# Local attention in pairs of 58-query blocks on half the partitions, in natural row order

## The chip, the cores and the metric

The kernel runs on one core of one Trainium2 chip. The metric is the time of one execution on the device in microseconds (us). The clock that the chip grants to TensorE varies from run to run (1.00 is the full clock). An execution that is more than 1.5% above the fastest of its kernel is called slow. The engines are PE (TensorE), DVE (VectorE), ACT (ScalarE), POOL (GpSimd) and SP, which here only issues transfers.

## The reference

```python
# q, k, v: 8 batches x 8 heads x 576 rows x 64, float32
q_d, k_d, v_d = means of q, k, v over groups of 4 rows          # 144 coarse rows
out_up    = repeat(softmax(q_d k_d^T / 8) v_d, 4)               # coarse attention
mask      = abs(i - j) < 4
out_local = softmax(where(mask, q k^T / 8, -1e9)) v             # local attention
x         = (out_up + out_local) as 8 x 576 x 512
wq, wk    = x @ w_q, x @ w_k                                    # 512 -> 64
mixed     = (wq wk^T / 8) x
out       = relu(mixed) @ w_out                                 # 8 x 576 x 512
```

## The kernel before

Eight batches go through four software stages: *cast* (to fp16, on POOL), *a* (transposes, coarse sums, local scores), *b* (probabilities times v, coarse attention, adding the two), *c* (the mixer, done as (x wq)(wk^T x), and the output product). Stages c, b and a of three successive batches, and the cast of the next, are interleaved in one program, and a scheduler orders each engine's instructions.

The queries are split into blocks of 120 rows, each with the 128 keys that it needs. The block's rows lie in *phase order*: all rows 0 mod 4 first, then 1 mod 4, and so on, so that one coarse row serves four stretches of the block.

```python
TQ = [30, 30, 30, 30, 24]; QN = [4 * t for t in TQ]; KS = [0, 116, 236, 356, 448]
# setup: masks, pooling matrices and selectors, with affine selects on GpSimd
for n in (0, 1, 4):                                  # one mask serves blocks 1, 2, 3
    asel(m3, [[-1, 4], [-4, TQ[n]]], ALU.is_ge, 0.0, OFF[n] + 3, 1)
    asel(m3, [[1, 4], [4, TQ[n]]], ALU.is_ge, 0.0, 3 - OFF[n], -1)
for n in (0, 1, 4): ...                              # P likewise: two selects each
for n in range(NW): asel(sel[n] ..., ALU.not_equal, 1.0, ...)    # one select each
[...]
def evac():                                          # q's transposed copy: DVE
    nc.vector.tensor_copy(qT[:, :, :, 0:128], pq16 ...)          # 4 phases x 144
def evack():                                         # k's: ACT, natural order
    nc.scalar.copy(kT[:, :, 0:512] ..., pk16 ...)
[...]
def sums():                                          # GpSimd
    nc.gpsimd.tensor_tensor(tq, qT[:, :, 0:2, :], qT[:, :, 2:4, :], op=ALU.add)
    nc.gpsimd.tensor_tensor(qd, tq[:, :, 0, :], tq[:, :, 1, :], op=ALU.add)
    nc.gpsimd.tensor_tensor(tk, k4[:, :, :, 0:2], k4[:, :, :, 2:4], op=ALU.add)
    ...                                              # kd from tk: five small adds
def score(n):                                        # five blocks
    for hl in range(NP):
        for p in range(2):                           # 64x128 weights, 120 columns
            nc.tensor.matmul(p_[:, p, hl * W:(hl + 1) * W],
                             kT[64 * p:64 * p + 64, hl, KS[n]:KS[n] + 128],
                             qT[64 * p:64 * p + 64, hl, :, 30 * n:30 * n + TQ[n]], ...)
    nc.scalar.activation(e_, p_[:, :, 0:4 * W], ACTF.Exp, scale=s_local)
    nc.vector.tensor_tensor(e8, e8, mask_n broadcast over 8 heads, op=ALU.mult)
[...]
def og(i):                                           # output, two of these a batch
    c = 120 * (2 * i + ff)
    nc.tensor.matmul(p_[0:120, ff, :], rmx[:, r, c:c + 120], wo16[:, r, :], ...)
    [...]                                            # copy, then DMA of 4-row groups
```

The *mask product* is `E = E * mask` on DVE, two operands in SBUF, 960 columns (768 in the last block), five times a batch.

The softmax here doesn't subtract the row's maximum and nothing guards it: scores larger than these inputs give would overflow.

Of the kernel before, what the change touches and what calls it, by code (L numbers as in the profile page):

```python
# [19 lines left out]
def kernel(  # L20
# [20 lines left out]

    NW = 5
    TQ = [30, 30, 30, 30, 24]
    QN = [4 * t for t in TQ]
    KS = [0, 116, 236, 356, 448]
    OFF = [KS[n] - 120 * n for n in range(NW)]

# [18 lines left out]
    def load(b):  # L66
# [10 lines left out]
        for n in range(NW):  # L77
            nc.sync.dma_start(v32[:, n], _ap(vb, KS[n] * D, [[D, 128], [S * D, H], [1, D]]))
# [16 lines left out]
    for n in (0, 1, 4):  # L95
        t_ = cst.tile([128, QN[n]], FP16, name=f"mask{n}")
        nc.vector.memset(t_, 1.0)
        m3 = t_.rearrange("p (f t) -> p f t", f=4)
        asel(m3, [[-1, 4], [-4, TQ[n]]], ALU.is_ge, 0.0, OFF[n] + 3, 1)
        asel(m3, [[1, 4], [4, TQ[n]]], ALU.is_ge, 0.0, 3 - OFF[n], -1)  # L100
        masks[n] = t_
# [3 lines left out]
    P = {}  # L105
    for n in (0, 1, 4):
        t_ = cst.tile([128, 32], FP16, name=f"P{n}")
        nc.vector.memset(t_, 0.0)
        u_ = t_[:, 0:TQ[n]]
        nc.vector.memset(u_, 0.25)  # L110
        asel(u_, [[-4, TQ[n]]], ALU.is_ge, 0.0, OFF[n], 1)
        asel(u_, [[4, TQ[n]]], ALU.is_ge, 0.0, 3 - OFF[n], -1)
        P[n] = t_
    P[2] = P[3] = P[1]
# [7 lines left out]

    sel = []
    for n in range(NW):
        t_ = cst.tile([128, 128], FP16, name=f"sel{n}")
        nc.vector.memset(t_, 0.0)
        asel(t_[:, 0:QN[n]].rearrange("p (f t) -> p f t", f=4), [[0, 4], [-1, TQ[n]]],
             ALU.not_equal, 1.0, 0 if n == 4 else -30 * n, 1)
        sel.append(t_)
# [3 lines left out]
    for i in range(2):  # L133
# [3 lines left out]
        es = []  # L137
        for n in range(NW):
            t_ = cst.tile([128, H * QN[n] + 32], FP16, name=f"E{n}_{i}")
            nc.vector.memset(t_[:, H * QN[n]:], 0.0)  # L140
            es.append(t_)
# [3 lines left out]
        for n in range(4):  # L145
            asel(t_[32 * n:32 * n + 32, :, 64], [[0, H]], ALU.is_ge, 0.0, 29, -1)
# [6 lines left out]
        asel(o_, [[0, 2], [32, 4]], ALU.is_ge, 0.0, 23, -1)  # L153
# [32 lines left out]
    def stage_a(b):  # L186
# [13 lines left out]
        def evac():  # L200
            qT = g["qT"] = big.tile([128, NP, 4, T], FP16, name="qT", tag="qT")
            nc.vector.tensor_copy(qT[:, :, :, 0:128],
                                  g["pq16"].rearrange("p a (j f t) -> p (a j) f t", j=2, f=4))

        def evack():
            kT = g["kT"] = big.tile([128, NP, S], FP16, name="kT", tag="kT")
            nc.scalar.copy(kT[:, :, 0:512].rearrange("p j (t f) -> p j t f", f=4),  # L207
                           g["pk16"].rearrange("p a (j f t) -> p (a j) t f", j=2, f=4))

        def rem():  # L210
            qT, kT = g["qT"], g["kT"]
            pr = ps(FP16, "pr")
            for j in range(NP):
                nc.tensor.transpose(pr[:, 0, 128 * j:128 * j + 128],
                                    g["r16"][:, 2 * j:2 * j + 2, :], id16)
            nc.vector.tensor_copy(qT[:, :, :, 128:T],
                                  _ap(pr, 0, [[row(pr), 128], [128, NP], [1, 4], [4, 16]]))
            nc.scalar.copy(kT[:, :, 512:S], _ap(pr, 64, [[row(pr), 128], [128, NP], [1, 64]]))

        def sums():  # L220
            qT, kT = g["qT"], g["kT"]
            tq = big.tile([128, NP, 2, T], FP32, name="tq", tag="tq", bufs=1)
            qd = g["qd"] = big.tile([128, NP, T], FP16, name="qd", tag="qd")
            nc.gpsimd.tensor_tensor(tq, qT[:, :, 0:2, :], qT[:, :, 2:4, :], op=ALU.add)  # L224
            nc.gpsimd.tensor_tensor(qd, tq[:, :, 0, :], tq[:, :, 1, :], op=ALU.add)  # L225
            tk = big.tile([128, NP, T, 2], FP32, name="tk", tag="tq", bufs=1)
            k4 = kT.rearrange("p j (t f) -> p j t f", f=4)
            kd = kdS[b % 2]
            nc.gpsimd.tensor_tensor(tk, k4[:, :, :, 0:2], k4[:, :, :, 2:4], op=ALU.add)  # L229
            for j in range(NP):  # L230
                nc.gpsimd.tensor_tensor(  # L231
                    kd[:, j, 0:128].rearrange("p (n t) -> p n t", n=4)[:, :, 0:30],
                    tk[:, j, 0:120, 0].rearrange("p (n t) -> p n t", n=4),
                    tk[:, j, 0:120, 1].rearrange("p (n t) -> p n t", n=4), op=ALU.add)
            nc.gpsimd.tensor_tensor(kd[:, :, 128:152], tk[:, :, 120:T, 0], tk[:, :, 120:T, 1],
                                    op=ALU.add)


        def score(n):
            def f_():  # L240
                qT, kT = g["qT"], g["kT"]
                W = QN[n]
                p_ = ps(name="psc")
                for hl in range(NP):
                    for p in range(2):
                        nc.tensor.matmul(p_[:, p, hl * W:(hl + 1) * W],  # L246
                                         kT[64 * p:64 * p + 64, hl, KS[n]:KS[n] + 128],
                                         qT[64 * p:64 * p + 64, hl, :, 30 * n:30 * n + TQ[n]],
                                         start=True, stop=True)
                E = E_S[b % 2][n]  # L250
                e_ = E[:, 0:H * W].rearrange("p (a c) -> p a c", a=2)
                nc.scalar.activation(e_, p_[:, :, 0:4 * W], ACTF.Exp, scale=s_local)  # L252
                e8 = E[:, 0:H * W].rearrange("p (h c) -> p h c", h=H)
                nc.vector.tensor_tensor(  # L254
                    e8, e8, _ap(masks[n], 0, [[row(masks[n]), 128], [0, H], [1, W]]), op=ALU.mult)
            return f_

        def vd():
# [8 lines left out]
            for p in range(2):  # L267
# [4 lines left out]

        return [(.9, tr("q16")), (0, evac), (.9, tr("k16")), (0, evack), (.25, rem), (0, sums),
                (.3, score(0)), (.3, score(1)), (.3, score(2)), (.3, score(3)), (.3, score(4)),
                (.5, vd)]

    def stage_b(b):
# [33 lines left out]
        def ca(i):  # L311
            def f_():
# [5 lines left out]
                lo, hi = ((0, 128), (120, T))[i]  # L318
# [18 lines left out]
        def av(n):  # L337
            def f_():
                if n == 0:
                    g["rz"] = big.tile([128, NW, 2, 4], FP32, name="rz", tag="rz")  # L340
                rz, W, E, v16 = g["rz"], QN[n], E_S[b % 2][n], g["v16"]
                p_ = ps(name="pav")
                for h in range(H):
                    c = ((h % 2) * 4 + h // 2) * W
                    nc.tensor.matmul(p_[:, h // 4, 65 * (h % 4):65 * (h % 4) + 65],  # L345
                                     E[:, c:c + 128], v16[:, n, h, :], start=True, stop=True)
                nc.vector.reciprocal(rz[0:W, n], _ap(p_, 64, [[row(p_), W], [512, 2], [65, 4]]))  # L347
                x_ = g["x"][n] = big.tile([128, DM], FP16, name=f"x{n}", tag=f"x{n}")
                nc.vector.tensor_tensor(
                    _ap(x_, 0, [[row(x_), W], [256, 2], [64, 4], [1, 64]]),  # L350
                    _ap(p_, 0, [[row(p_), W], [512, 2], [65, 4], [1, 64]]),
                    _ap(rz, 8 * n, [[row(rz), W], [4, 2], [1, 4], [0, 64]]), op=ALU.mult)
            return f_

        def up(n):
            def f_():
                W, x_ = QN[n], g["x"][n]
# [3 lines left out]
                nc.vector.tensor_tensor(x_[0:W], x_[0:W], pu[0:W, 0, :], op=ALU.add)  # L361
# [164 lines left out]
```

## Time and profile before

| | before |
|---|---|
| median of 3 runs | 253.94 us (253.6 to 254.33) |
| profiled run | 255.02 us, span 253.3 us, granted clock 0.869 |
| distance between M2 products (one a batch), full batches | 25.7, 25.8, 27.1, 29.0, 25.2 us |
| 40 mask products | 53.3 us |
| first cast of q begins | 7.72 us |

"M2 product" is the first `pm` matmul of a batch on PE. It closes each batch's chain, so the distance from one to the next is the batch's period. The first lies at 57.78 us (the head), the last at 234.67, 18.6 us from the end (the tail).

One batch of before, from its timeline (columns: start us, duration us, engine, line, operation, out<-in, count, and in brackets the idle time before it with what ended it):

```profile
91.42 1.40 POOL L225 TENSOR_TENSOR qd<-tq 128x576 f16<-128x576 f32 x1
91.88 1.45 DVE L254 TENSOR_TENSOR E_1_176<-E_1_176,mask_91 128x960 f16<-128x960 f16 x1 [0.21 <-ACT E_1_176 L252]
...
92.90 2.40 POOL L229 TENSOR_TENSOR tk<-kT 128x1152 f32<-128x1152 f16 x1
...
93.97 1.84 DVE L254 TENSOR_TENSOR E_1_178<-E_1_178,mask_95 128x960 f16<-128x960 f16 x1
...
97.34 2.83 POOL L174 CAST q_1129<-q_1028 128x2048 f16<-128x2048 f32 x1
97.77 0.65 DVE L254 TENSOR_TENSOR E_1_180<-E_1_180,mask_95 128x960 f16<-128x960 f16 x1
...
98.93 1.75 DVE L254 TENSOR_TENSOR E_1_182<-E_1_182,mask_95 128x960 f16<-128x960 f16 x1
...
102.33 0.54 DVE L254 TENSOR_TENSOR E_1_184<-E_1_184,mask_99 128x768 f16<-128x768 f16 x1
...
107.10 0.64 ACT L396 CAST wT<-pw 128x576 f16<-128x576 f32 x1 [0.57 <-PE pw L393]
107.84 1.22 DVE L202 COPY qT<-pq_1454 128x2048 f16<-128x2048 f16 x1 [1.85 <-PE pq_1454 L196]
108.46 0.42 ACT L405 COPY wk<-pwk 96x320 f16<-96x320 f16 x1 [0.72 <-PE pwk L403]
```

The same 960-column product takes 0.65 us or 1.45 to 1.84 us.

### The profile page before, as it was taken

The numbers are of one execution on the slowest core, as the hardware profiler recorded it, in microseconds if no ns is written. First come the engines' busy times: TensorE is split into PE (matmuls) and PEld (weight loads), VectorE is DVE, ScalarE is ACT, GpSimd is POOL, SyncE is SP. The second block draws the span as 40 slices with busy tenths as digits, with TensorE's granted clock in tenths as the row PEclk, the third lists the DMA queues.
The fourth block names the chain that finished last, engine by engine and source line by source line (L and its number), as shares of the span: only waits on it lengthen the run. The fifth ranks groups of instructions, "written<-read, shape, count | busy, mean of one in ns | idle before, by whom it ended". The sixth has DMA issues, their size and how long they took to land.

```text
span 253.3 us, 4685 instructions
## 1 busy us (share of the span) xinstructions
PE 182.3 (72%) x1856; PEld 115.2 (45%) x1856; DVE 177.4 (70%) x320; ACT 110.9 (44%) x153; POOL 137.3 (54%) x140
## 2 busy tenths in 40 slices
PE   0430786498988885888769866887788977996890
PEld 0330563266546643565337533554455544553340
DVE  7148499337895889578995899579977995754210
ACT  2081345035455554556343741556355546212310
POOL 8979939920999099708960599009960920000000
PEclk9995586559589999999799987899999799979568
DMA  6999999999227992699349961797330033024015
GB/s 209 254 241 363 219 241 265 213 306 183 44 78 195 304 194 80 176 310 196 91 111 318 182 160 32 232 263 163 89 100 4 1 97 93 0 44 145 0 25 161
DMA packets 71366, 40.41 MB, mean 160 GB/s; under 512 B 51760, under 2 KB 68144, under 8 KB 71344
## 3 DMA queue, kind: packets, MB, share of 16 engines
q1 hardware_dynamic: 71344, 40.11, 65.8%
q8 instruction: 14, 0.23, 0.4%
q14 instruction: 8, 0.07, 0.1%
HBM read 30.67 MB, written 9.44 MB: 158 GB/s over the span
## 4 chain that ended last, share of the span: by engine, by line
PE 41%; DVE 26%; ACT 13%; POOL 13%; issue 4%; ACTq 0%; POOLq 0%
PE po L448 6%; ACT kT L207 4%; PE pw L393 4%; DVE os L453 3%; PE pol L463 3%; ACT rmx L435 3%; PE px L374 3%; PE pmx L426 2%; DVE E_1_178 L254 2%; POOL tk L229 2%; POOL tq L224 2%; DVE E_1_176 L254 2%; PE pav L345 2%; ACT Ec L295 2%; DVE E_1_182 L254 2%
## 5 line engine op out<-in xcount | busy, mean ns | idle before, releaser
L224 POOL TENSOR_TENSOR tq<-qT 128x1152 f32<-128x1152 f16 x8 | 18.9, 2363 | 64.4 <-DVE rz L347 58.6
L448 PE MATMUL po<-wo_90,rmx 128*120 128x512 f16 x128 | 39.0, 461 | 0.6 <-ACT os L451 0.4
L448 PEld LDWEIGHTS <-rmx 128*120 128x120 f16 x128 | 20.1, 162 | 15.1 <-issue 8.6
L246 PE MATMUL psc<-qT,kT 64*128 64x120 f16 (+1 forms) x320 | 16.2, 228 | 7.3 <-ACT rmx L435 2.5
L229 POOL TENSOR_TENSOR tk<-kT 128x1152 f32<-128x1152 f16 x8 | 19.2, 2400 | 0.6
L246 PEld LDWEIGHTS <-kT 64*128 64x128 f16 x320 | 10.8, 100 | 18.2 <-issue 15.0
L437 DVE TENSOR_SCALAR rmx<-pmx 128x576 f16<-128x576 f32 x16 | 12.0, 748 | 8.4 <-PE pmx L431 8.2
L463 PE MATMUL pol<-wo_90,rmx 128*96 128x512 f16 x32 | 10.1, 408 | 7.7 <-DVE os L453 7.7
L451 ACT COPY os<-po 120x1024 f32<-120x1024 f32 x8 | 8.1, 1012 | 16.3 <-PE po L448 16.3
L393 PE MATMUL pw<-xT,wqk_89 128*128 128x288 f16 x64 | 11.5, 306 | 4.7 <-ACT Ec L295 3.6
L453 DVE COPY os<-po 120x1024 f32<-120x1024 f32 x8 | 9.7, 1215 | 6.3 <-PE po L448 6.3
L435 ACT ACTIVATE rmx<-pmx 128x576 f16<-128x576 f32 x16 | 10.4, 653 | 6.6 <-PE pmx L431 6.6
L465 ACT COPY ol<-pol 96x512 f32<-96x512 f32 x8 | 4.7, 582 | 18.5 <-PE pol L463 18.5
L377 DVE COPY xT<-px 128x1152 f16<-128x1152 f16 x16 | 11.9, 750 | 1.0 <-PE px L374 0.6
L225 POOL TENSOR_TENSOR qd<-tq 128x576 f16<-128x576 f32 x8 | 11.5, 1440 | 0.5
L295 ACT ACTIVATE Ec<-pcs 128x576 f16<-128x576 f32 x16 | 9.7, 649 | 2.5 <-PE pcs L291 2.5
L231 POOL TENSOR_TENSOR kd_149<-tk 128x120 f16<-128x120 f32 x16 | 9.6, 624 | 0.2
L329 DVE RECIPROCAL rc<-pca 128x8 f32<-128x8 f32 (+1 forms) x16 | 3.2, 201 | 8.5 <-PE pca L326 8.5
L393 PEld LDWEIGHTS <-wqk_89 128*128 128x128 f16 x64 | 5.8, 103 | 7.4 <-DVE vblk_192 L268 2.5
L196 PE MATMUL pq_224<-id_64,q_202 128*128 128x128 f16 x16 | 1.9, 312 | 9.7 <-POOL q_202 L174 9.7
L254 DVE TENSOR_TENSOR E_0_151<-E_0_151,mask_91 128x960 f16<-128x960 f16 x4 | 6.6, 1662 | 2.7 <-ACT E_0_151 L252 2.7
L347 DVE RECIPROCAL rz<-pav 120x8 f32<-120x8 f32 (+1 forms) x40 | 7.1, 189 | 2.0 <-PE pav L345 1.9
(597 smaller groups left out, 577.2 us busy)
## 6 DMA issues: line engine op xcount, KB each, us to landing
out_dram<-os SPq DMA_DIRECT2D x16, 480.0 KB, 3.4
out_dram<-ol SPq DMA_DIRECT2D x8, 192.0 KB, 3.1
v_72<-in_v_dram SPq DMA_DIRECT2D x5, 256.0 KB, 5.5
v_214<-in_v_dram SPq DMA_DIRECT2D x5, 256.0 KB, 6.5
v_356<-in_v_dram SPq DMA_DIRECT2D x5, 256.0 KB, 5.4
v_653<-in_v_dram SPq DMA_DIRECT2D x5, 256.0 KB, 5.3
v_1031<-in_v_dram SPq DMA_DIRECT2D x5, 256.0 KB, 6.2
v_1409<-in_v_dram SPq DMA_DIRECT2D x5, 256.0 KB, 5.4
```

The source lines that it names most:

```text
L224: nc.gpsimd.tensor_tensor(tq, qT[:, :, 0:2, :], qT[:, :, 2:4, :], op=ALU.add)
L229: nc.gpsimd.tensor_tensor(tk, k4[:, :, :, 0:2], k4[:, :, :, 2:4], op=ALU.add)
L246: nc.tensor.matmul(p_[:, p, hl * W:(hl + 1) * W], kT[64 * p:64 * p + 64, hl, KS[n]:KS[n] + 128], qT[64 * p:64 * p + 64, hl, :, 30 * n:30 * ...
L254: nc.vector.tensor_tensor(e8, e8, _ap(masks[n], 0, [[row(masks[n]), 128], [0, H], [1, W]]), op=ALU.mult)
L295: nc.scalar.activation(g["Ec"][:, i].rearrange("p a c t -> p a (c t)"), p_[:, :, 0:2 * T], ACTF.Exp, scale=s_coarse)
L377: nc.vector.tensor_copy(g["xT"][:, 2 * i:2 * i + 2, :], p_[:, :, 0:S])
L393: nc.tensor.matmul(p_[:, i, 0:288], wqk16[:, r, :], xT[:, r, 288 * i:288 * i + 288], start=(r == 0), stop=(r == 3))
L435: nc.scalar.activation(d_, s_, ACTF.Relu)
L437: nc.vector.tensor_scalar_max(d_, s_, 0.0)
L448: nc.tensor.matmul(p_[0:120, ff, :], rmx[:, r, c:c + 120], wo16[:, r, :], start=(r == 0), stop=(r == 3))
L453: nc.vector.tensor_copy(os_, p_[0:120])
L463: nc.tensor.matmul(p_[0:96, 0, :], rmx[:, r, 480:S], wo16[:, r, :], start=(r == 0), stop=(r == 3))
```

## The change

Its intent: 58 queries need only 64 keys, so two such blocks share the 128 partitions, each on its half. Scores, exponentials and mask products then work on 2304 columns a batch in place of 4608. All rows go to natural order, so that q's copy can look like k's and the output is written in 128-row tiles.

```diff
-    TQ = [30, 30, 30, 30, 24]
-    KS = [0, 116, 236, 356, 448]
+    WQ = [58, 58, 58, 58, 56]
+    Q0 = [...]; K0 = [min(max(q0 - 3, 0), S - 64) for q0 in Q0]     # ten halves
+    PAIRS = [(0, 3), (1, 2), (4,)]
[...]
-    for n in (0, 1, 4):                 # P: two selects each; sel: one each
+    for n in range(NW):                 # P, sel: every pair its own, on each half
+        for c ...: asel(...); asel(...) # four small selects each
[...]
-            nc.vector.tensor_copy(qT[:, :, :, 0:128], pq16 ...)     # DVE
+                nc.scalar.copy(t_[:, :, 0:512] ..., g["p" + key] ...)   # q and k: ACT
[...]
-                for hl in range(NP):
-                    for p in range(2):
-                        nc.tensor.matmul(p_[:, p, ...], kT[..., KS[n]:KS[n] + 128], qT[...])
+                for i, n in enumerate(pr_):
+                    for hl in range(NP):
+                        for p, c in ((0, 0), (1, 1), (0, 1), (1, 0)):
+                            nc.tensor.matmul(p_[64 * c:64 * c + 64, p, o:o + w],
+                                             kT[64 * p:64 * p + 64, hl, K0[m]:K0[m] + 64],
+                                             qT[64 * p:64 * p + 64, hl, Q0[m]:Q0[m] + w],
+                                             tile_position=(64 * p, 64 * c))
[...]
+                if pr_ == (1, 2):       # one mask: one product of 928 columns
+                    e_ = [(1, E ...)]
+                else:                   # (0, 3): two products of 464; (4,): one of 448
+                    e_ = [(n, E[:, :, i, :, 0:w]) for i, n in enumerate(pr_)]
+                for n, t_ in e_:
+                    nc.vector.tensor_tensor(t_, t_, mask_n broadcast, op=ALU.mult)
[...]
-                        c = 120 * (2 * i + ff)
-                        nc.tensor.matmul(p_[0:120, ff, :], rmx[:, r, c:c + 120], wo16[:, r, :])
+                        c = 128 * (2 * i + ff)
+                        nc.tensor.matmul(p_[:, ff, :], rmx[:, r, c:c + 128], wo16[:, r, :])
```

## The prediction

> **What bounds it now.** No engine is full: on the page PE is busy 72% of the span, DVE 70%, POOL 54%, ACT 44%. The chain of work that ended last is PE 41%, DVE 26%, ACT 13%, POOL 13%. In order of time: up to about 47 us it is nearly all POOL (setup selects, casts, sums). Then come six batches with all three stages, 25.2 to 29.0 us apart. Each has about 10 us limited by latency (xT, wT, wk, M2, kT evacuation, rmx, passing between PE and ACT), then about 15 us in which DVE never rests (115.5 to 130.9). Last, a tail of 40 us has no scores. In the window 106 to 133 DVE is busy 23.0 of 27 us, PE 21.4, POOL 15.8, ACT 13.7.
>
> **What the change does, per batch.**
> - Exp on half the width: five activations, 4.7 us (0.97 each, 0.81 the last), become three, about 2.4.
> - Mask products: 4608 columns become 2320. One of 960 columns takes 0.55 to 0.84 us when POOL reads nothing beside it, 1.2 to 1.85 when it does. The Trainium skill ("SBUF — State Buffer", Who interferes with whom) says that a DVE instruction with two SBUF inputs contends with a GpSimd one that reads SBUF; these durations agree. The waiting part goes with the number of products (5 to 4), not their width: I estimate 6.7 us down to 4.2.
> - qT evacuation moves from DVE (1.22 us) to ACT (1.87, as kT's shows); kT's remainder (0.37) from ACT to DVE. DVE in all about -3.3 us, ACT -0.7.
> - PE: scores and probabilities-times-v go from 80 to 160 matmuls in 64x64 tiles. Eight of the old took 0.40 to 0.43 us. The eight 64x32 tiles for the coarse remainder took 0.26, so tiles overlap, but twice the instructions and weight loads (the skill, "TensorEngine Tiling (Array Packing)", Restrictions: column tiling disables fast weight load) I estimate at +1.5 to 2 us. The mixer saves four small matmuls.
> - v comes in ten half-width transfers in place of five, same bytes: about a us more DMA, hidden.
>
> **On the critical path.**
> 1. The 15 us DVE part shrinks by 2.5 to 3 us, less than DVE's full saving, as PE's extra work lies there.
> 2. The qT evacuation now stands on ACT between wT and wk. wk started 0.7 us after wT's end; it will start about 1.8 after. This is on the chain: +1.0 us a batch.
> 3. Affine selects ahead of POOL's first cast rise from 29 to 63. At 0.16 to 0.26 us each, the first cast moves from 7.7 to about 12.5 us, and the POOL-bound head with it: +4.5 us. DVE's setup grows too (E memsets), hidden under this.
> Net: six batches x 1.7, plus 2 us from the earlier ones, minus 4.5: about -8 us.
>
> **Prediction: 246 us, 239 to 252. Faster by over 2%: 0.62; within 2%: 0.30; slower by over 2%: 0.08.**
>
> **What would show it.** POOL's timeline: first q cast near 12.5 us. A middle batch: period near 24.3 us, DVE busy 19 to 20. ACT's timeline: qT evacuation between wT and wk; PE's wait for wk up by 1 us. Groups: mask products about 34 us in all (53 before), exp 19 (37 before).
>
> **What would make it wrong.** If 64x64 tiles don't overlap, or switching modes drains PE, PE becomes the limit and nothing is gained. If POOL and the mask products collide less, a batch falls to 22 us and the time below 239. If loads were the hidden limit, shorter batches would wait for v.

## More of the kernel before

From the page of the kernel before: the span, the busy time of each engine (instructions behind the x), the chain of work that ended last by engine, and the group of q's coarse sums (busy us, mean ns, then the idle time before it and what ended that).

```profile
span 253.3 us, 4685 instructions
...
PE 182.3 (72%) x1856; PEld 115.2 (45%) x1856; DVE 177.4 (70%) x320; ACT 110.9 (44%) x153; POOL 137.3 (54%) x140
...
PE 41%; DVE 26%; ACT 13%; POOL 13%; issue 4%; ACTq 0%; POOLq 0%
...
L224 POOL TENSOR_TENSOR tq<-qT 128x1152 f32<-128x1152 f16 x8 | 18.9, 2363 | 64.4 <-DVE rz L347 58.6
```

No engine is full. The chain passes from engine to engine, so a saving counts only where it stands on the chain.

## The result, and the profile after

The median is 250.36 us (249.48 to 251.18, 4 runs) against 253.77 (253.06 to 254.33, 4 runs) of before on the same chip: ratio 0.9866, 95% interval 0.982 to 0.9913: the change is faster, by 0.9 to 1.8%. A ratio here is the mean time of one kernel's fast runs over that of the other's fast runs of the same rounds, so it is not quite the ratio of the two medians. The forecast was -7.9 us; the result is -3.4.

From the page of the changed kernel, the same lines, with the chain by line added:

```profile
span 248.1 us, 5991 instructions
...
PE 170.3 (69%) x2464; PEld 99.1 (40%) x2464; DVE 169.7 (68%) x328; ACT 105.3 (42%) x137; POOL 129.4 (52%) x179
...
DVE 34%; PE 32%; ACT 13%; SPq 9%; issue 6%; DMA 2%; POOL 2%; ACTq 0%; DVEq 0%
PE po L482 5%; DVE E_1_229 L285 5%; SPq L83 4%; DVE E_0_208 L285 4%; PE pw L429 3%; SPq L79 3%; DVE xT L413 3%; ACT qT L224 2%; ACT rmx L469 2%; DVE E_1_231 L285 2%; PE pmx L463 2%; DVE os L487 2%; PE pca L353 2%; DMA v_263<-in_v_dram 2%; ACT wk L442 1%
```

Every engine is less busy, and DVE's share of the chain has risen, with mask products (L285) high on the list. PE fell too, although its matmuls went from 1856 to 2464. The 9% of SPq and 2% of DMA are new: in the head the chain now runs along the issuing of transfers, where v has ten in place of five. That is a rival for the longer head. But issuing v for the first batch took 9.28 us against 8.08, for the second 9.11 against 9.75, and e13 below shortens the head without touching the transfers.

One batch of the changed kernel, from its timeline (same columns):

```profile
173.28 0.68 DVE L285 TENSOR_TENSOR E_0_208<-E_0_208,mask_96 128x464 f16<-128x464 f16 x1 [0.28 <-ACT E_0_208 L274]
173.78 2.14 POOL L245 TENSOR_TENSOR sum_2867<-kT 128x1152 f32<-128x1152 f16 x1
173.88 2.30 DVE L285 TENSOR_TENSOR E_0_208<-E_0_208,mask_102 128x464 f16<-128x464 f16 x1
...
177.71 2.31 POOL L202 CAST v_2553<-v_2184 128x2560 f16<-128x2560 f32 x1
...
178.73 1.79 DVE L285 TENSOR_TENSOR E_0_210<-E_0_210,mask_102 128x928 f16<-128x928 f16 x1
180.03 2.23 POOL L195 CAST q_2757<-q_2635 128x2048 f16<-128x2048 f32 x1
...
181.03 1.47 DVE L285 TENSOR_TENSOR E_0_212<-E_0_212,mask_108 128x448 f16<-128x448 f16 x1
...
186.89 0.69 ACT L432 CAST wT<-pw 128x640 f16<-128x640 f32 x1 [0.62 <-PE pw L429]
...
187.78 1.87 ACT L224 COPY qT<-pq_3124 128x2048 f16<-128x2048 f16 x1 [0.20 <-PE pq_3124 L217]
...
189.54 0.48 ACT L442 ACTIVATE wk<-pwk,rows 128x256 f16<-128x256 f16 x1
```

The second product of pair (0, 3) has half the columns of a product of before and takes 2.30 us: it begins 0.10 us after the 2.14 us sum of k and ends 0.26 us after it (176.18 against 175.92). It takes 2.30 us in all eight batches (minimum, median, maximum in ns, from the instructions of the product's line):

```profile
L285 DVE TENSOR_TENSOR E_0_208<-E_0_208,mask_102 x4: 2299/2299/2301, 26.4 to 173.9; 128x464 f16<-128x464 f16 x4
...
L285 DVE TENSOR_TENSOR E_1_229<-E_1_229,mask_102 x4: 2298/2302/2306, 46.4 to 199.4; 128x464 f16<-128x464 f16 x4
```

In the two batches shown, both at a granted clock of 1.00, the five products of before add up to 6.23 us and the four of after to 6.24. Over the run they are 53.3 us (40 products) and 45.8 us (32).

Where the time went, in the profiled runs, with a second trace of before (experiment e16) beside it, since before's own traces differ by 2.5 us:

| stretch, us | before, two traces | after | difference | forecast |
|---|---|---|---|---|
| start to first cast of q | 7.72 / 7.70 | 16.16 | +8.4 | +4.8 |
| first cast of q to first M2 product | 50.1 / 50.8 | 46.2 | -3.8 / -4.6 | -2 |
| five full batches, mean of one | 26.57 / 25.95 | 25.54 | -1.0 / -0.4 | -1.7 |
| sixth batch | 24.5 / 25.9 | 23.9 | -0.6 / -2.0 | -1.7 |
| seventh to eighth M2 product | 19.5 / 17.9 | 17.5 | -2.0 / -0.4 | 0 |
| tail | 18.6 / 18.8 | 16.6 | -2.0 / -2.1 | 0 |
| span | 253.3 / 250.8 | 248.1 | -5.2 / -2.7 | -7.9 |

Among the batches at a granted clock of 1.00 the gain is smaller still: 25.79 and 25.19 us in before, 25.20 and 25.42 in after.

The head, first cast of q on POOL, before:

```profile
7.72 1.89 POOL L174 CAST q_202<-q_69 128x2048 f16<-128x2048 f32 x1
```

and after, with two of the lines ahead of it (x2 and x4 are the instructions that one line joins):

```profile
13.92 0.42 POOL L60 TENSOR_SCALAR_AFFINE_SELECT sel_192<-sel_192 128x56 f16<-128x56 f16 x2
14.30 0.70 POOL L60 TENSOR_SCALAR_AFFINE_SELECT rows<-rows 64x1 f32<-64x1 f32 x4
...
16.16 1.89 POOL L195 CAST q_251<-q_69 128x2048 f16<-128x2048 f32 x1
```

### The profile page after: what moved, and what is told of

The parts are those of the page before. It is cut to its first block, busy times and chain, and to the rows that moved or that the text cites. A ratio compares the mean times of both kernels' runs of the same rounds, so it can differ in the third digit from the quotient of the medians.

```text
span 248.1 us, 5991 instructions
## 1 busy us (share of the span) xinstructions
PE 170.3 (69%) x2464; PEld 99.1 (40%) x2464; DVE 169.7 (68%) x328; ACT 105.3 (42%) x137; POOL 129.4 (52%) x179
## 4 chain that ended last, share of the span: by engine, by line
DVE 34%; PE 32%; ACT 13%; SPq 9%; issue 6%; DMA 2%; POOL 2%; ACTq 0%; DVEq 0%
PE po L482 5%; DVE E_1_229 L285 5%; SPq L83 4%; DVE E_0_208 L285 4%; PE pw L429 3%; SPq L79 3%; DVE xT L413 3%; ACT qT L224 2%; ACT rmx L469 2%; DVE E_1_231 L285 2%; PE pmx L463 2%; DVE os L487 2%; PE pca L353 2%; DMA v_263<-in_v_dram 2%; ACT wk L442 1%
## 5 line engine op out<-in xcount | busy, mean ns | idle before, releaser
L482 PE MATMUL po<-wo_95,rmx 128*128 128x512 f16 x128 | 36.4, 437 | 0.2 <-ACT os L485 0.2
L482 PEld LDWEIGHTS <-rmx 128*128 128x128 f16 x128 | 13.3, 110 | 19.2 <-issue 9.3
L385 DVE RECIPROCAL rz<-pav 128x8 f32<-128x8 f32 x40 | 7.9, 198 | 17.1 <-PE pav L380 17.0
L269 PE MATMUL psc<-qT,kT 64*64 64x58 f16 (+1 forms) x640 | 10.2, 202 | 9.5 <-DVE x_2027 L387 2.0
L485 ACT COPY os<-po 128x1024 f32<-128x1024 f32 x8 | 8.1, 1012 | 17.1 <-PE po L482 17.1
L429 PE MATMUL pw<-xT,wqk_94 128*128 128x320 f16 x64 | 11.4, 300 | 4.5 <-DVE vblk_220 L299 1.6
L269 PEld LDWEIGHTS <-kT 64*64 64x64 f16 x640 | 7.7, 116 | 15.7 <-issue 4.7
L413 DVE COPY xT<-px 128x1280 f16<-128x1280 f16 x16 | 12.9, 814 | 1.2 <-PE px L411 1.2
L487 DVE COPY os<-po 128x1024 f32<-128x1024 f32 x8 | 9.7, 1214 | 5.9 <-PE po L482 5.9
L285 DVE TENSOR_TENSOR E_1_229<-E_1_229,mask_102 128x464 f16<-128x464 f16 x4 | 9.2, 2302 | 0.0
L285 DVE TENSOR_TENSOR E_0_208<-E_0_208,mask_102 128x464 f16<-128x464 f16 x4 | 9.2, 2300 | 0.0
```

Of the source, the lines that this page charges most:

```text
L269: nc.tensor.matmul(p_[64 * c:64 * c + 64, p, o:o + w], kT[64 * p:64 * p + 64, hl, K0[m]:K0[m] + 64], qT[64 * p:64 * p + 64, hl, Q0[m]:Q0[m ...
L285: nc.vector.tensor_tensor(t_, t_, _ap(m_, 0, [[row(m_), 128]] + bc + [[1, w]]), op=ALU.mult)
L385: nc.vector.reciprocal(rz[:, n], _ap(p_, 64, [[row(p_), 128], [512, 2], [65, 4]]))
L413: nc.vector.tensor_copy(g["xT"][:, 2 * i:2 * i + 2, :], p_[:, :, 0:640])
L429: nc.tensor.matmul(p_[:, i, 0:320], wqk16[:, r, :], xT[:, r, 320 * i:320 * i + 320], start=(r == 0), stop=(r == 3))
L482: nc.tensor.matmul(p_[:, ff, :], rmx[:, r, c:c + 128], wo16[:, r, :], start=(r == 0), stop=(r == 3))
```

## The experiments

All ran on one core; each of the groups e1 to e4, e5 to e8, e9 to e12 and e13 to e16 shared a chip and its runs of before (medians 254.32, 255.05, 253.95 and 254.45 us), so compare across groups by the ratios. "Period" is the mean distance of M2 products over the five full batches. "Clean batch" is one without a disturbance, with a granted clock of 1.00. Times and ranges are those of all runs, slow ones too; ratios are those of the fast runs alone. "Products" is the sum of the durations of the mask products.

The tail needs care. The profiled runs e1, e2 and e12 end 12.6 to 12.7 us after the last M2 product, at a granted clock of 0.93 to 1.00 there; after, e3, e4, e5 and e9 take 16.3 to 16.9, at 0.70 to 0.71. So up to 4 us between two runs of the changed kind can be the clock of the tail, and the period is the safer figure.

| run | time, us (range) | ratio to before, 95% | first M2 | period | products, us |
|---|---|---|---|---|---|
| after | 250.36 (249.5–251.2) | 0.9866 (0.982–0.9913) | 62.38 | 25.54 | 45.8 |
| e1 one product | 238.91 (234.8–241.7) | 0.927 (0.916–0.9381) | 62.15 | 24.12 | 30.1 |
| e2 qT on DVE | 248.06 (245.3–252.6) | 0.9654 (0.9556–0.9752) | 62.60 | 25.19 | 46.9 |
| e3 short sums | 244.85 (244.0–245.5) | 0.9618 (0.9553–0.9683) | 62.63 | 24.75 | 33.2 |
| e4 mask on PE, wrong | 233.9 (232.4–239.8) | 0.9174 (0.9091–0.9258) | 61.01 | 23.85 | none |
| e5 head | 250.48 (247.7–252.1) | 0.9727 (0.965–0.9804) | 63.09 | 25.81 | 45.5 |
| e6 before, short sums | 241.19 (237.4–242.8) | 0.9373 (0.9271–0.9475) | 59.16 | 24.00 | 39.1 |
| e7 mask on PE | 238.72 (234.7–238.9) | – (one fast run) | 60.66 | 23.54 | none |
| e8 e7 + head + qT on DVE | 237.85 (237.2–242.1) | 0.9329 (0.9271–0.9387) | 63.81 | 23.32 | none |
| e9 head, ordered | 249.09 (249.0–249.8) | 0.9828 (0.9779–0.9877) | 60.81 | 25.79 | 45.7 |
| e10 120 rows, wrong | 251.83 (251.0–253.6) | 0.9939 (0.987–1.0008) | 62.63 | 26.79 | 48.5 |
| e11 e3 + qT on DVE | 242.6 (239.5–244.6) | – | 63.42 | 24.17 | 32.7 |
| e12 e7 + ordered head | 232.54 (230.0–235.7) | 0.9136 (0.9056–0.9216) | 57.91 | 24.14 | none |
| e13 fewer selects, wrong | 243.97 (241.8–245.1) | 0.9589 (0.9457–0.9721) | 57.10 | 25.55 | 45.3 |
| e14 before, mask on PE | 238.11 (234.1–238.4) | – (one fast run) | 52.88 | 24.56 | none |
| e15 before, qT on ACT | 261.11 (259.0–266.1) | 1.0242 (1.0135–1.035) | 58.19 | 27.59 | 51.6 |
| e16 before again | 253.5 (252.5–257.6) | 0.9958 (0.987–1.0046) | 58.50 | 25.95 | 49.1 |

### e1: the products of pair (0, 3) written as one

```diff
+    m03 = cst.tile([128, 2, 2, NP, WQ[0]], FP16, name="m03")    # both masks, written out
[...]
+                if pr_ == (0, 3):
+                    nc.vector.tensor_tensor(t_, t_, m03 ..., op=ALU.mult)   # 928 columns
```

> The changed kernel with one edit: the two mask products of the block pair (0,3), 464 columns each, become one of 928 columns against a mask tile written out in full at setup. The elements multiplied stay the same. Theory A (the mask products wait on the vector engine while a GpSimd instruction reads SBUF, and the gap between the two products hands the port to the 2.1 us sum of kT): the product that took 2.30 us in all eight batches is gone, the joined one takes 0.65 to 0.9 us, mask products fall from 45.7 to about 33 us in all, the six full batches shorten by 1 to 2 us each, total 239 to 245 us. Rival B (a batch is limited by the hand-overs between PE and ACT, and the vector engine's waiting is slack): products fall just as much, the total moves by less than 2 us from 250.

Measured: correct, 238.91 us, the products 30.1 us in all, the period 1.4 us shorter. The same columns are multiplied by eight instructions fewer, and 15.7 us of product time are gone, 2.0 us for each. What cost the time was that a product stood right behind another just as POOL's sum of k began. In seven of the eight batches the joined product begins ahead of that sum and takes 0.65 to 1.42 us; in the eighth it begins 0.09 us after it and takes 2.52, so theory A's 0.65 to 0.9 us was met in one batch alone. Two batches side by side:

```profile
94.38 0.65 DVE L287 TENSOR_TENSOR E<-E,m 128x928 f16<-128x928 f16 x1 [0.34 <-ACT E L277]
94.40 2.59 POOL L248 TENSOR_TENSOR sum<-kT 128x1152 f32<-128x1152 f16 x1
...
118.41 2.11 POOL L248 TENSOR_TENSOR sum<-kT 128x1152 f32<-128x1152 f16 x1
118.50 2.52 DVE L287 TENSOR_TENSOR E<-E,m 128x928 f16<-128x928 f16 x1 [0.34 <-ACT E L277]
```

In these two, whichever begins first runs at its own pace, and the other lasts longer. Some of the fall in the median is the clock of the tail (12.7 us), so the period is the safer figure.

### e2: q's transposed copy back on DVE

```diff
-                nc.scalar.copy(t_[:, :, 0:512] ...)
+                put = nc.vector.tensor_copy if dst == "qT" else nc.scalar.copy
+                put(t_[:, :, 0:512] ...)
```

> The changed kernel with the evacuation of qT put back on the vector engine (1.2 us there, 1.87 us on ACT), all else kept. Theory A (the evacuation stands on ACT between wT and wk, on the chain): wk starts about 0.7 to 1.0 us after the end of wT in place of 2.0, the period of the full batches falls by 0.7 to 1.1 us, total about 243 to 245 us. Rival B (only the mask products' port lock matters, ACT has slack there): period unchanged within 0.3 us, total 249 to 251.

Measured: correct, 248.06 us, period only 0.35 us shorter. The wait was removed: wk begins 0.89 us after wT's end (110.71 to 111.60), in after it was 2.0. But the copy to natural order takes 2.29 us on DVE, where before's copy to phase order took 1.22, and DVE's next reciprocals begin later for it. The Trainium skill ("VectorE: DVE Perf Modes", Mode 2×_1P) says that two results a cycle need 16-bit tensors with a step of one; the natural order is read from PSUM with a step of 128, and the factor of 1.9 agrees. The gain turned into another wait. The fast runs (245.32 and 246.1 us) look better than the period: in the profiled one the tail is 12.6 us against after's 16.6, at a granted clock of 0.94 against 0.71. They don't show that the copy is worth 4 us.

### e3: each long POOL sum cut in four

```diff
-                nc.gpsimd.tensor_tensor(s_, t4[:, :, :, 0:2], t4[:, :, :, 2:4], op=ALU.add)
+                for j in range(NP):
+                    nc.gpsimd.tensor_tensor(s_[:, j], t4[:, j, :, 0:2], t4[:, j, :, 2:4], op=ALU.add)
```

> The changed kernel with each of the two large GpSimd sums (2.1 us) cut into four of a quarter the size. Nothing is taken off any engine; GpSimd gains some fixed cost, about 0.3 to 0.6 us a batch. Theory A (a mask product waits for the end of the one GpSimd instruction that holds the port): the product of 2.30 us falls to about 0.9 to 1.1 us, since the instruction it waits for is a quarter as long; total 243 to 248. Rival C (the product is slow by its own access pattern, or bandwidth is shared between the engines): it stays near 2.3 us, since the same bytes are read beside it.

Measured: correct, 244.85 us. POOL works more (137.0 us against 129.4, or 0.95 us a batch, above the expected 0.3 to 0.6) and the kernel is faster: the products fall from 45.8 to 33.2 us and the period by 0.8, with neither their number nor their width changed. One batch of e3 from its timeline:

```profile
95.26 1.87 DVE L286 TENSOR_TENSOR E<-E,mask 128x464 f16<-128x464 f16 x2 [0.28 <-ACT E L275]
96.17 2.73 POOL L246 TENSOR_TENSOR sum<-kT 128x288 f32<-128x288 f16 x4
...
99.68 0.73 DVE L286 TENSOR_TENSOR E<-E,mask 128x928 f16<-128x928 f16 x1
...
100.93 2.31 POOL L202 CAST v<-v 128x2560 f16<-128x2560 f32 x1
101.58 1.91 DVE L286 TENSOR_TENSOR E<-E,mask 128x448 f16<-128x448 f16 x1 [0.15 <-ACT E L275]
```

The pair's two products take 1.87 us from the first's start to the second's end (2.90 in after), and the 928-column one 0.73. The smallest product of all, 448 columns, now takes 1.91: it runs into the cast of v, which is still one instruction of 2.31 us, and ends 0.25 us after it. Waiting time goes with the POOL instruction that a product meets.

### e4: the mask added on PE, no products (wrong result)

```diff
-                nc.vector.tensor_tensor(t_, t_, mask ..., op=ALU.mult)
+  # ahead of the scores: identity x mask into PSUM, mask = 0 or -30000, then add the scores
+                nc.tensor.matmul(p_[:, p, ...], id16, mask ..., start=True, stop=False)
-                             start=True, stop=True, tile_position=...)
+                             start=False, stop=True, tile_position=...)
```

> The changed kernel with no mask product at all: a mask of 0 and -30000 is put into PSUM by an identity matmul ahead of the scores, which accumulate onto it; exp then gives zero outside the band. The vector engine loses 45.7 us of products in all (5.7 us a batch), PE gains 16 matmuls a batch of 224 to 464 columns, estimated 1.0 to 1.3 us. Theory A (the products with their waits hold back the vector engine, which is the chain of the second half of a batch): periods fall from 25.5 to about 22 to 23 us, total 228 to 236. Rival B (hand-overs between PE and ACT limit a batch): total 246 to 252, as PE's extra work cancels what is gained.

Measured: 233.9 us, but the result is wrong (relative error 0.488). In pair (0, 3) two mask matmuls with start=True go to the same PSUM bank. The Trainium skill ("PSUM — Partial Sum Buffer", Terms, the entries on has_written and the zero region) says that such a matmul clears the written bits of the whole bank in the quadrants of partitions that it writes (here all four), so the scores of the first half overwrite the mask instead of adding to it. e7, where only the first matmul of a bank starts, is correct, which agrees.

### e5: the setup by ramps and compares (the head)

```diff
-            asel(u_, [[-4, hi - lo]], ALU.is_ge, 0.0, off, 1)          # 63 selects ahead of the cast; 7 are left
-            asel(u_, [[4, hi - lo]], ALU.is_ge, 0.0, 3 - off, -1)
+    Dm = iota(...); Dp = iota(...); Ds = iota(...)                       # three on GpSimd
+            nc.vector.tensor_scalar(x_, d_, lo, v, op0=ALU.is_ge, op1=ALU.mult)
+            nc.vector.scalar_tensor_tensor(out_, d_, hi, x_, op0=ALU.is_le, op1=ALU.mult)
```

> The changed kernel with its constants made another way: three number ramps on GpSimd, and the masks, pooling matrices, selectors and row masks by pairs of compare instructions on VectorE; the steady state is untouched. The selects ahead of GpSimd's first cast of q fall from 63 to the few of the identity. Theory (the head's extra time is the chain of small selects ahead of the first cast, 16.16 us in after against 7.72 before): the first cast of q starts at 8 to 9 us, the first M2 product at 57 to 58.5 us instead of 62.38, and the time falls by 4 to 5 us below the 250.4 of after, to 245 to 247. Rival (the head is set by loads or by VectorE, the selects are hidden): the first M2 product moves by less than 1.5 us and the time by less than 1.5. Periods of the full batches stay at 25.5 on average, mask products at 45.7 us.

Measured: correct; first cast of q at 6.39 us, 9.8 us earlier than in after, and yet the first M2 product at 63.09, later than after's 62.38. By the ratios (0.9727 against 0.9866, on different chips, intervals close to overlapping) the time fell by about 1.4%. The profiled run was slow. POOL's timeline shows where the gain went:

```profile
22.19 1.02 POOL L60 TENSOR_SCALAR_AFFINE_SELECT vd<-vd 32x8 f16<-32x8 f16 x4 [9.92 <-DVE vd L175]
23.27 0.59 POOL L60 TENSOR_SCALAR_AFFINE_SELECT vblk<-vblk 128x8 f16<-128x8 f16 x2
23.81 2.24 POOL L255 TENSOR_TENSOR sum<-qT 128x1152 f32<-128x1152 f16 x1
```

POOL stands 9.92 us for a fill that DVE reaches only after its new compares. The work moved and its wait came along. This run neither shows nor refutes the theory of the head.

### e6: the kernel before with its POOL sums cut in four

```diff
-            nc.gpsimd.tensor_tensor(tq, qT[:, :, 0:2, :], qT[:, :, 2:4, :], op=ALU.add)
+            for j in range(NP):
+                nc.gpsimd.tensor_tensor(tq[:, j], qT[:, j, 0:2, :], qT[:, j, 2:4, :], op=ALU.add)
   # the same for tk
```

> The kernel BEFORE, with each of its two long GpSimd sums over head dimensions cut in four instructions, one per row block. Theory (a mask product with two SBUF inputs waits as long as the GpSimd instruction that holds the shared port, in before as in after): its 40 mask products fall from 53.4 us to 37 to 41, its full-batch mean falls from 26.57 by 0.5 to 1.2 us, and the time from 254 to 246 to 251. Then the change itself, with short sums in both kernels, is worth 244.85 against that: a few us. Rival (before loses nothing to the port; only the changed kernel has the collision): products stay above 50 us and the time within 1 us of before.

Measured: correct, 241.19 us, ratio 0.9373: one loop around two instructions of before gains more than the whole change. Products 53.3 to 39.1 us, period 24.00. The profiled run was slow (clock 0.883), which can only make this look worse. So the collision belongs to both kernels. With short sums in both, the changed kernel is the slower one: by the ratios (0.9618 against 0.9373), and by the clean batch, which takes 24.57 us against 23.24 in before (two batches alike; a third at that clock took 24.47). Up to the second xT copy they are level (19.38 and 19.17 us after the M2 product); then the changed kernel needs 4.66 us until wk, before 3.22.

### e7: the mask on PE, mended

```diff
-                                         start=True, stop=False, ...)
+                                         start=(i == 0), stop=False, ...)    # once per bank
```

> The additive-mask experiment with its error mended: only the first matmul in a PSUM bank starts the accumulation, the score matmuls add to it. Expected correct. Theory (the 5.7 us a batch that VectorE spends in mask products is on the critical path, and most of it is waiting for GpSimd, so taking the products away altogether gives more than writing them as one): DVE busy 130 to 132 us, full-batch mean 23.6 to 24.1, time 231 to 236. Rival (PE's added mask matmuls and the slower start of the scores eat the gain): full-batch mean above 24.6, time above 240.

Measured: correct, one fast run of 234.74 us (three slow ones at 238.7 to 238.9), period 23.54, clean batch 23.20. DVE is busy 130.6 us. The chain, from its page:

```profile
PE 51%; ACT 14%; SPq 13%; issue 6%; POOL 5%; DVE 5%; DMA 3%; ACTq 0%
```

With the products gone, DVE is no longer what limits. e4 (fast runs 232.4 to 234.8) agrees in time, though its numbers were wrong.

### e8: mask on PE, setup as in e5, q's copy on DVE

The edit is e7, e5 and e2 together.

> Three reasons at once: additive mask on TensorE, constants by ramps and compares, and q's transposed copy on VectorE instead of ScalarE. If the parts add: 233.5 minus 4.5 for the head and 0 to 2 for the copy, 227 to 230 us, correct. If VectorE is no longer what ends last once the products are gone, the copy gives nothing or costs, and only the head's part is seen: 229 to 233.

Measured: correct, fast runs 237.2 to 237.9 us. A miss: the parts do not add. The first M2 product is at 63.81 us for the reason found in e5, and q's copy moved the period by only 0.2 us from e7's 23.54. But four of e7's five full batches had a clock of 1.00 and only three of e8's. The clean batches went from 23.20 to 22.67 and 22.73, so once the products are gone the copy is better on DVE, by about 0.5 us a batch. No run has it together with e12's head.

### e9: the head again, with the fills ordered

```diff
+    # ramps and compares as in e5, and: vd and vblk of both sets are filled ahead of everything
+    # else on DVE; selectors, row masks and the second set are made after the first merge [...]
-                nc.vector.tensor_copy(t_[:, :, 512:S], ...)
+                put = nc.scalar.copy if b == 0 else nc.vector.tensor_copy
+                put(t_[:, :, 512:S], ...)
```

> The head again. In the first attempt the casts began 9.8 us earlier but GpSimd then stood 9.9 us behind VectorE's setup, so the sums began at 23.8 us (22.9 in after). Here the tiles that GpSimd writes in its setup are filled first on VectorE, and the remainder of qT and kT of the first batch is copied by ScalarE, so that GpSimd waits for nothing of VectorE's late setup. Theory (the head is GpSimd's chain, selects then casts then sums then the v cast, as long as nothing else delays it): first q cast at 7 to 8.5 us, first sum at 14 to 15.5, v cast ended at 25 to 27 us instead of 33.7, first M2 product at 56.5 to 59 instead of 62.4, time 3.5 to 5.5 us below after's. Rival (loads or VectorE's setup set the head whatever GpSimd does): first M2 product stays above 61 us.

Measured: correct, 249.09 us; cast of v ended at 27.83 us instead of 33.73, but the first M2 product at 60.81, between the two theories. POOL is now early and DVE is late: after its compares and fills it reaches the first mask products at 28.36 us (25.44 in after). So the remake on DVE costs most of what it saves on POOL: of 9.9 us at the first cast, 1.6 arrive at the first M2 product.

### e10: 120 columns and rows in the output product (wrong)

```diff
-                        nc.tensor.matmul(p_[:, ff, :], rmx[:, r, c:c + 128], wo16[:, r, :], ...)
+                        nc.tensor.matmul(p_[0:120, ff, :], rmx[:, r, c:c + 120], wo16[:, r, :], ...)
   # the copies and the DMA on 120 of 128 rows likewise: 8 rows of each tile are not written
```

> The changed kernel, wrong on purpose: its output products take 120 columns of the mixer rows as weights, as before did, and 120 of each 128 output rows are written. It asks where the 4 us at the end come from (sixth to last M2 product 17.5 us in every changed kernel, 19.5 in before; last M2 product to the end 16.6 against 18.6). Theory (weights of 120 columns load slower, 0.152 to 0.162 us against 0.110, and in the last two stages, where PE runs alone, this is on the chain): weight loads at 0.15 us, that last distance back at 19 or more, time 2 to 4 us above after's. Rival (it comes from the output's row order and the shorter last transfer, or from the clock): last distance stays at 17.5, time within 1 us of after.

Measured: 251.83 us, ratio 0.9939, with two batches of 28.8 us in the profiled run (their granted clock is 0.88; the other three have 0.93 to 1.00). The weight loads went from 110 to 148 ns, near before's 162. But the distance between the last two M2 products stayed at 17.5 us, so my theory fell: slower weight loads are hidden there. What did move is the wait at the very end, for the last output transfer. Before, after, and e10, from the waits of the queue that issues the transfers (us in all, times, longest):

```profile
SPq L521 <- DMA out_dram<-ol: 4.0, 1, 4.0
```

```profile
SPq L555 <- DMA out_dram<-ol: 2.2, 1, 2.2
```

```profile
SPq L555 <- DMA out_dram<-ol: 3.7, 1, 3.7
```

The last transfer itself is the same in after and e10; only the larger ones ahead of it went from 128 to 120 rows. The wait is 4.0 to 4.2 us in every trace of before's kind and 2.2 to 2.4 in every other trace of the changed kind. So about 1.5 us of the tail's 2 come from the 128-row output tiles.

### e11: short sums, and q's copy on DVE

The edit is e3 and e2 together.

> The changed kernel with short GpSimd sums and with q's transposed copy put back on VectorE. With short sums in both, a clean batch of the changed kernel takes 24.57 us and one of before 23.25: of the 1.3 us, 1.4 lie between the second xT copy and the end of wk, where q's copy stands on ScalarE. Theory (that copy, on ScalarE's chain, is what makes the changed kernel's batch longer; in before it stood on VectorE in 1.85 us of idle time): wk within 1.0 us of wT's end, clean batches at 23.3 to 23.9 us, time 240 to 243. Rival (the natural-order copy takes 2.29 us on VectorE and delays the next reciprocals and products as much as it frees): clean batches at 24.2 or more, time 243.5 to 246.

Measured: correct, fast runs 239.5 and 241.1 us, clean batches 24.45 against 24.57 in e3. The theory fell for the period: taking the copy off ACT brought wk forward by 0.9 us relative to the second xT copy, and the 2.29 us copy on DVE put the first add back by 0.6. The two fast times lie in the theory's range or below it, but the profiled tail was 14.0 us against e3's 16.3. Beside the mask products the copy costs about the same on either engine, now that it gathers into natural order.

### e12: mask on PE with the ordered head

The edit is e7 and e9 together, q's copy on ACT.

> Additive mask on TensorE together with the ordered head, q's copy left on ScalarE. If the parts add: 234.7 (the fast run of the mask on TensorE) minus 3 to 5 us of head: 229.5 to 232, correct, first M2 product at 55 to 58 us, full-batch mean 23.3 to 23.8. If the first stages were full of something else, the first M2 product stays at 60.7 and the time at 234 to 236.

Measured: correct, 232.54 us (fast runs 229.99, 232.52, 232.56), ratio 0.9136. First M2 product 57.91, 2.75 us earlier than in e7, of the 9.7 us by which the first cast is earlier. The rest of its lead over e7's one fast run can't be told from the clock: its tail is 2.5 us shorter, its five full batches 3.0 us longer (three of them at 0.93). This is the version that beats both kernels, by 8.6% and, by the two ratios to before, by about 7% over the changed one.

### e13: 24 selects fewer (wrong)

```diff
     for n in range(NW):
+        if n in (1, 2, 3):
+            P.append(P[0]); continue            # the same for sel
```

> The changed kernel, wrong on purpose: the pooling matrix and the selector of pair 0 stand in for those of pairs 1, 2 and 3, so 24 selects are gone from GpSimd (at 0.21 to 0.24 us each, about 5.3 us) and no work is put anywhere else. Theory (the head's added time is the selects): first q cast at 10.5 to 11.3 us instead of 16.16, first M2 product at 58.5 to 60.5 instead of 62.38, time 2 to 4 us below after's 250.4. Rival (the head has other limits behind the selects, as the two remakes suggest): first M2 product above 61.5.

Measured: wrong (error 0.055), 243.97 us, ratio 0.9589. Nothing was added anywhere, and the theory holds, stronger than expected. POOL's timeline, first cast of q (16.16 in after):

```profile
10.64 1.89 POOL L201 CAST q<-q 128x2048 f16<-128x2048 f32 x1
```

The cast comes 5.5 us earlier, the first M2 product 5.3 us earlier (57.10), the period is unchanged (25.55). So in the changed kernel 5.3 of the 5.5 us that POOL loses ahead of the first cast are paid by the whole kernel.

### e14: the kernel before with the mask on PE

```diff
+                    nc.tensor.matmul(p_[:, p, 0:NP * W], id16, mask_n ..., start=True, stop=False)
-                                         start=True, stop=True)
+                                         start=False, stop=True, ...)
-                nc.vector.tensor_tensor(e8, e8, mask_n ..., op=ALU.mult)
```

> The kernel BEFORE with the mask added on TensorE and no mask products. Against the changed kernel with the same edit (full-batch mean 23.54 and 23.85 in two traces, 232.8 fast span) it says what the pairing is worth once the mask products are out of both. Theory (the products were the only part of the change that could shorten VectorE's stretch, so nothing is left): full-batch mean 22.5 to 23.8, time 232 to 238. Rival (half the exp, fewer PSUM columns and cheaper PE still give a gain): full-batch mean above 24.3, time above 240.

Measured: correct, one fast run of 234.11 us, level with e7's 234.74. Period 24.56, clean batch 24.18, so my theory's range was missed and the rival's figure for the period met, not its time. The clean batch is 0.98 us longer than e7's, and it adds 4608 mask columns on PE where e7 adds 2304: the mask matmuls are busy 22.6 us there and 12.6 in e7, 1.25 us a batch. That fits a pairing that pays for itself on PE in this form of the kernel, though no run changes the mask's columns alone; but the kernel before has its first M2 product 7.8 us earlier, with its fewer selects, and the two ends cancel.

### e15: the kernel before with q's copy on ACT

```diff
-            nc.vector.tensor_copy(qT[:, :, :, 0:128], pq16 ...)
+            nc.scalar.copy(qT[:, :, :, 0:128], pq16 ...)
```

> The kernel BEFORE with one part of the change: q's transposed copy on ScalarE. In before this copy of 1.22 us ran on VectorE after 1.85 us without work, outside the stretch where VectorE never rests. Theory (moving it frees VectorE where it had time anyway and puts 1.9 us between wT and wk): wk 1.8 to 2.1 us after wT's end instead of 0.72, full-batch mean 0.3 to 1.2 us longer than before's 26.6, time 1 to 6 us longer. Rival (VectorE's 1.2 us a batch are worth what the forecast took them for): time 1 to 5 us shorter.

Measured: correct, 261.11 us, ratio 1.0242: one part of the change, done alone, costs 1.3 to 3.5% (on record as unclear, as the interval spans 2%). ACT's timeline:

```profile
167.58 0.64 ACT L396 CAST wT<-pw 128x576 f16<-128x576 f32 x1 [0.57 <-PE pw L393]
168.31 1.86 ACT L202 COPY qT<-pq 128x2048 f16<-128x2048 f16 x1
170.07 0.42 ACT L405 COPY wk<-pwk 96x320 f16<-96x320 f16 x1
```

wk begins 1.85 us after wT's end (168.22 to 170.07), 0.72 in before. DVE's stretch begins no earlier: the first add of the coarse part comes 6.19 us after the M2 product in the clean batches of both. The period is 1.6 us above e16's, but not in the clean batches. These take 26.00 and 25.24 us, where e16 has 25.99 and 25.19 in the same places: in the last of them the wait of 1.1 us is there, and the batch's products happen to take 1.1 us less (5.96 against 7.06 in before). The loss lies in the three other batches, of 31.9, 27.8 and 27.0 us, at granted clocks of 0.84, 0.94 and 0.87. So the run shows the wait, and that nothing is gained; why the whole kernel loses 1.3 to 3.5% stays open.

### e16: the kernel before again

> The kernel before, unchanged, for a second trace. Expected: the products 53 to 54 us, and between the last two M2 products 19.3 to 19.6 us again if those 2 us belong to the kernel, 17.5 if they were luck of the clock. Ratio within 1% of 1.

Measured: 253.5 us. Products 49.1 us, 4.2 less than in the first trace, and 17.9 us between the last two M2 products. So most of the 2 us that the first pair of traces showed there was luck: in the first trace one group of eight output matmuls took 3.56 us in place of 1.89, in 3.4 us at a granted clock of 0.50. It is also a warning on reading one trace: before's period is 26.57 or 25.95.

## Why the prediction was right or wrong

**The step that failed: "The waiting part goes with the number of products (5 to 4), not their width: I estimate 6.7 us down to 4.2."** Measured: 53.3/8 = 6.7 down to 45.8/8 = 5.7, and 6.23 to 6.24 in the two clean batches. The work in a product did shrink: unblocked, before's five take 4 x 0.645 + 0.545 = 3.1 us, after's four 2 x 0.38 + 0.63 + 0.38 = 1.8 (shortest of each form in the runs). So the waiting was 3.6 us a batch (3.0 in before's second trace, with 49.1 us of products) and is 3.9 now. It did not fall at all. A blocked product lasts until the POOL instruction ends, plus 0.25 us for 448 or 464 columns, 0.41 for 768 or 0.5 for 928 or 960. In the 13 traces with mask products, 321 of these take over 1.3 times the unhindered time of their form, and every one ends so, within 0.02 us. So its length is set by when that instruction ends. The Trainium skill ("SBUF — State Buffer", SBUF: two separate sides) calls the shared port pair an exclusive lock: of a DVE instruction with two SBUF inputs and a GpSimd one that reads SBUF, the one that starts first has it for its whole instruction, and the other blocks fully. The two batches shown under e1 agree, but the start that the profile shows is not exactly when the pair is taken: in 14 of 440 products of these traces a product runs unhindered inside a POOL instruction that began up to 0.44 us before it, and that instruction is the one that lasts longer (a cast of q 2.83 us in place of 1.89). I had cited that page, and then spread the waiting evenly over the products, which the lock does not do. e3 shows it (same products, shorter POOL instructions, -12.6 us of product time), e6 shows it for before, e1 shows the particular collision, of the second (0, 3) product with the sum of k.

**The DVE part "shrinks by 2.5 to 3 us".** In the clean batches, from the first add of the coarse part to the second xT copy, it went from 15.5 to 14.05 us. The 1.5 us are not the products. They come mostly from idle gaps that closed (1.0 us of them in before, 0.3 in after) and from one multiplication by rz that now runs ahead of that stretch. The forecast's full DVE saving of 3.3 us also held q's copy of 1.2, which stood in DVE's idle time; in e15, without it, the stretch begins no earlier (6.19 us after the M2 product in both).

**q's copy between wT and wk, "+1.0 us a batch": right as a wait.** wk began 2.0 us after wT's end (0.72 before), and from the second xT copy to the next M2 product the clean batch went from 4.07 to 5.12 us, +1.05. Without the expected gain on DVE, this eats two thirds of what was left. What the copy's place is worth in the whole batch is less: in clean batches, putting it back on DVE gave 0.1 us in e11 (against e3) and 0.5 in e8 (against e7).

**The head: right in kind, its size wrong.** "The first cast moves from 7.7 to about 12.5": it moved to 16.16. That is arithmetic: in after 63 selects take from 1.08 to 16.16 us, 0.24 each, and 34 more of them are 8.1 us; even the prediction's own 0.16 to 0.26 gives 5.4 to 8.8, and it used 4.8. e13 shows that this time counts almost in full (5.3 of 5.5 us). "2 us from the earlier ones" were 3.8. Net +4.6 in place of +2.5.

**PE, "+1.5 to 2 us": wrong in sign.** In the clean batches PE went from 19.71 to 19.40 us with 308 matmuls instead of 232. Sixteen probability products took 0.44 us, eight of the old 0.42. The skill ("TensorEngine Tiling (Array Packing)", Restrictions) says that column tiling disables fast weight load. The trace has 116 ns for a weight load of 64x64 and 100 for the old 64x128 one, so a single load is no faster at half the size. Even so the 640 score matmuls are busy for 10.2 us where the 320 of before took 16.2.

**Not foreseen: the end.** The tail was 2 us shorter, 1.5 of it from the 128-row output tiles (e10, which refuted my own theory of slower weight loads).

Added up against the first trace of before: head +8.4 - 3.8, six batches -5.8 (forecast -10.2), the end -4.0, of which some 1.6 were luck of the clock. Against the second trace: head +3.9, six batches -4.0, the end -2.6. What stays open: why e15's batches at a lower clock are so long, and how much of the changed kernel's batch would be gained by a copy of q that is short on DVE.

## What to carry to other kernels

If a two-operand DVE instruction meets long GpSimd instructions, first cut those up or take the product away: halving its columns does nothing while it waits for a lock, and a loop around two sums of the old kernel gained 6%. Before counting an engine's saving, look where in the period it stands, since an instruction that runs in idle time gives nothing when it is moved and can cost where it lands. Count the small setup instructions ahead of the first piece of work: here nearly all of their time was paid by the whole kernel (e13), and moving them to another engine gave little of it back (e5, e9). And look at the granted clock of each stretch before reading a difference between two runs: here the tail alone varied by 4 us.

## What the Trainium skill lacked or had wrong

- "SBUF — State Buffer" has the rule of the lock, and that the one who waits does so for a whole instruction. It does not say what is left to do after that. Here a blocked product ended 0.25 us (448 or 464 columns) to 0.5 us (928 or 960) after the GpSimd instruction, 2.30 us in place of 0.38 in the worst place of each batch. Nor does it say that shorter GpSimd instructions are a remedy: cutting two 2.1 us sums into four each took 12.6 us off 32 products, though GpSimd itself worked 7.6 us longer.
- "TensorEngine Tiling (Array Packing)", Restrictions, says what column tiling disables and gives no time for it. Here 640 score matmuls in 64x64 tiles were busy 10.2 us, 320 with 64x128 weights 16.2, and the weight loads took 116 and 100 ns each.
- No page has the price of an affine select: 0.18 to 0.32 us on GpSimd, for 1 to 128 columns, on half the partitions or all of them. So two small selects cost well over one large one, and 63 in place of 29 ahead of the first cast moved that by 8.4 us.
